# mLSTM cell and feed-forward on one core: another hand-written order for the first chunk

## The chip, the core and the metric

The kernel runs on one core of a Trainium2 chip. The metric is the device time of one execution in microseconds (us). Below, PE is TensorE (matrix products), DVE is VectorE, ACT is ScalarE, POOL is GpSimd, and SP is SyncE, which here only issues transfers (DMAs). All engines run their own queues in order and wait for each other on semaphores.

## What is computed

An mLSTM cell (a gated linear recurrence over 768 positions, for 4 batches of 8 heads of size 40) feeds a feed-forward layer with a leaky ReLU over the 3072 tokens. The recurrence is written step by step in the reference; the kernel computes it in chunks.

```python
for t in range(S):                                  # S = 768; B = 4, H = 8, D = 40
    m_new = np.maximum(f_gate[:, :, t] + m, i_gate[:, :, t])
    f_stab = np.exp(f_gate[:, :, t] + m - m_new)
    i_stab = np.exp(i_gate[:, :, t] - m_new)
    C = f_stab[..., None, None] * C + i_stab[..., None, None] * np.einsum('bhd,bhe->bhde', vt, kt)
    n = f_stab[..., None] * n + i_stab[..., None] * kt
    denom = np.maximum(np.abs(np.einsum('bhd,bhd->bh', n, qt)), 1.0)
    y[:, :, t] = o * np.einsum('bhde,bhe->bhd', C, qt) / denom
x = y.transpose(0, 2, 1, 3).reshape(3072, 320)
h = x @ w_in                                        # 320 x 2048
out = np.maximum(0.01 * h, h) @ w_out               # 2048 x 320
```

The feed-forward weights arrive as 64-bit floats, which the kernel narrows to 32 bits itself with a row of DVE instructions.

## The kernel before

The 768 positions are cut into 6 chunks of 128. A *step* `s` is one batch of one chunk: steps 0 to 3 are chunk 0, steps 4 to 7 chunk 1, and so on. The feed-forward of chunk `g` runs on PE while the cell work of chunk `g+1` is slipped in between its units.

**The first chunk** has no feed-forward to lie beside. Its order is written out by hand in the string `ORDER`. Each word is a call (table `acts_of` in `first_chunk`), and PE, DVE, ACT and POOL run their instructions exactly in the order in which the words issue them. SP's transfers stand in that order too. The words that matter here:

- `ld s`, `lo s`, `lw n`: load k, q, v of a step; its output gate; block `n` of w_in as 64-bit numbers (blocks 0 to 3 are w_in). `fd s` and `ll s i` load for later steps.
- `g c`, `ge c`, `ug c`: gates of chunk `c` on DVE (L297 to L317), their exponentials on ACT, their transposes on PE (L347, L352) with the copy on DVE (L357).
- `ab`, `abw s`: PE spreads gate rows over the partitions (L472), DVE adds the mask (L482).
- `tr s i`, `tc s i`: PE turns k (i = 0) or q (i = 1) of a step (L595), ACT copies the result out of PSUM (L601).
- `sc s`, `exp s`, `scm s`: scores on PE (L610), eight exponentials on ACT (L499), their product on DVE (L617). `vu`, `st`, `stc`: the new state on POOL, PE (L625) and DVE (L633).
- `val s`, `den s`, `gate s`, `gp s`: values on PE (L690), denominator on DVE (L682 to L684), output gate on DVE (L702), division on POOL (L719).
- `x s`, `xc s`: PE turns the token rows (L893), ACT copies them into `xT` (L906, L907).
- `nw n`: the next of seven instructions that narrow weight block `n`: L264 on ACT, then L266, L268, L270, L275, L279, L281 on DVE. `nw 0 e` narrows one half of block 0. The feed-forward may read a block after its L281.
- `ff j b0 b1`: feed-forward unit `j` for the batches `b0` to `b1-1`: ten products of 64x128 weights with 128 columns a batch (L924), then two leaky ReLUs on ACT (L932).
- `warm n`: `n` spare products of the identity with itself (L340); nobody reads them.

**The feed-forward of chunk 0** follows, interleaved with the cell of chunk 1, and is 30 units: units 0 and 1 finish `ff 0` and `ff 1` for batches 2 and 3, units 2 to 13 are pairs of half units for j = 2 to 7 (six and four products of 512 columns), and units 14 to 29 are the second layer (L960), four products each. So unit 6 is the first that reads weight block 2, and unit 10 the first that reads block 3; unit 14 reads the blocks 4 and 5 (w_out), unit 26 the blocks 10 and 11. Three tuples set what goes between the units: `PASSES[i]` gives how many narrowing instructions are issued before unit `i`; `fetch` gives the unit ahead of which further blocks of w_out are loaded; `place[n]` gives the unit behind which the n-th cell part of chunk 1 is issued. These parts are `u_parts` (turns, scores and state sums of a step: L559, L667, L672, L677) and `u_plain` (values of a step, hN at L730, then den, gate and state), for steps 4 to 7, the gate transposes of chunk 2, and the turning of the four token rows (`u_x1`, L893).

PSUM is two sets of four banks: the feed-forward, the masks and the spare products take turns in one, the cell in the other.

```python
            run(now, PASSES[i])
            for n in fetch.get(i, ()):
                load_weights(QN + n)
            ...
            exps()
            ffs[i]()
            ...
            while done < min(len(cells), sum(p <= i for p in place)):
```

Of the kernel before, what the change touches and what calls it, by code (L numbers as in the profile page):

```python
# [22 lines left out]
def kernel(  # L23
# [53 lines left out]
    gp = ctx.enter_context(tc.tile_pool(name="gates", bufs=1))  # L77
# [283 lines left out]
    st = {}  # L361
# [721 lines left out]
    def run(steps, n=None):  # L1083

        for _ in range(H if n is None else n):
            next(steps, None)
# [34 lines left out]
            nc.tensor.matmul(st["warm"][:], lhsT=ident[:], rhs=ident[:], start=True, stop=True)  # L1121

    ORDER = """
ld 0; g 0; ld 1; ge 0; lo 0; lw 0; warm 3; warm 4
lo 1; ld 2; warm 1; warm 5; warm 1; ab 0; ug 0; ld 3
abw 0; lo 2; tr 0 0; tr 1 0; tc 1 0; tr 1 1; tr 0 1; abw 1
tc 0 1; tc 0 0; warm 3; sc 0; vu 0; vu 1; vu 2; lo 3
lw 1; o 0; tc 1 1; st 1; st 0; stc 1; exp 0; stc 0
scm 0; exp 1; warm 6; warm 3; sc 1; warm 3; scm 1; ab 2
val 0; g 1; abw 3; tr 2 0; tr 2 1; val 1; tr 3 0; tiles  # L1130
den 0; nw 0 1; gate 0; nw 0 0; abw 2; tc 2 0; tc 2 1; ge 1
o 1; vu 3; tc 3 0; exp 2; warm 4; sc 2; ps 0; gp 0
ps 1; gate 1; nw 0 0; nw 0 0; den 1; scm 2; ug 1; nw 0 1
nw 0 1; o 2; tr 3 1; warm 4; val 2; x 0; tc 3 1; exp 3
nw 0 0; warm 3; st 2; xc 0; nw 1; gate 2; den 2; sc 3
stc 2; st 3; nw 0 0; nw 0 0; scm 3; nw 0 0; nw 0 1; fd 4
gp 2; ll 4 1; ps 2; gp 1; lw 2; warm 5; x 1; val 3
nw 0 1; xc 1; o 3; den 3; gate 3; nw 0 1; nw 0 1; nw 1
stc 3; nw 1; warm 3; ff 0 0 2; x 2; gp 3; lw 3; ps 3
fd 5; ll 5 1; ll 4 2; x 3; xc 2; xc 3; lw 4; ll 5 2  # L1140
lw 5; fd 6; nw 1; nw 1; nw 1; fd 7; lw 6; ff 1 0 2
sp 4; spc 4; nw 1
"""

    def first_chunk():

        ffs, narrow = [], {}

        def ff(j, b0, b1):
            if not ffs:  # L1150
                ffs.extend(ff_units(0))
            ffs[0](j, b0, b1)

        def step(n, e=None):
            if (n, e) not in narrow:
                narrow[n, e] = narrow_weights(n, e)
            next(narrow[n, e], None)

        acts_of = {
            "ld": load, "lo": load_o, "lw": load_weights, "g": gates, "ge": gates_exp, "warm": warm,  # L1160
            "ug": lambda c: gates_T(c, bus[c][0] if c == 0 else bus.pop(c)[0]),
            "tr": u_transpose, "tc": transpose_copy, "ab": lambda n: spread_first(bus[0][1], n), "abw": spread_mask,
            "exp": lambda n: run(prep_exp(n)), "vu": prep_vu, "tiles": prepare_tiles, "sc": u_scores, "scm": scores_mix,
            "st": state, "stc": state_copy, "val": u_values, "den": values_den, "o": prep_o, "gate": gate,
            "gp": gate_scale, "nw": step, "ps": prepare_step, "x": u_x, "xc": x_copy, "ff": ff,
            "sp": split_turn, "spc": split_copy, "warmer": warmer, "idle": idle, "fd": feed, "ll": load_late,
        }
        for line in ORDER.split("\n"):
            for what in line.split(";"):
                name, *args = what.split() or [None]  # L1170
                if name:
                    acts_of[name](*map(int, args))
        return ffs[1]

    E = mybir.EngineType
    with tc.manual_schedule(engines={E.PE, E.DVE, E.Activation, E.Pool}):
        ffs = first_chunk()
        fetch = {3: (3, 4), 13: (5, 6), 15: (7,)}
        PASSES = (5, 0, 3, 0, 0, 1, 7, 1, 0, 4, 3, 0, 1, 3, 10, 0, 1, 1, 3, 2, 9, 6, 0, 3, 3, 1, 7, 1, 2, 19)
        place = (1, 4, 8, 13, 15, 18, 20, 20, 23, 25, 26, 27, 27)  # L1180
        late = {}
        now = (None for n in range(2, QN + NF // 2) for _ in narrow_weights(n))

# [9 lines left out]
        for i in range(len(ffs)):  # L1193
            run(now, PASSES[i])
            for n in fetch.get(i, ()):
# [158 lines left out]
```

## Time and profile before

| | us |
|---|---|
| median of 3 runs | 481.94 (481.75 to 482.24) |
| the profiled execution | 481.68 |
| its span, first to last instruction | 479.5 |
| PE busy | 473.3 (99% of the span) |
| DVE busy | 365.6 (76%) |
| ACT busy | 199.9 (42%) |
| POOL busy | 162.1 (34%) |
| granted PE clock | 1.00 throughout |

What lies around the span is 481.68 - 479.5 = 2.2 us. By stages of the span:

| stage (us) | PE busy | DVE busy | ACT busy | POOL busy | share of the DMA engines |
|---|---|---|---|---|---|
| 0 to 10 | 8.20 | 5.03 | 2.27 | 5.10 | 0.73 |
| 10 to 20 | 9.51 | 6.55 | 8.04 | 0.85 | 1.02 |
| 20 to 30 | 10.00 | 8.22 | 8.43 | 5.90 | 0.98 |
| 30 to 40 | 9.74 | 9.44 | 5.28 | 4.17 | 0.84 |
| 40 to 50 | 10.00 | 9.72 | 9.65 | 5.92 | 1.10 |
| 60 to 70 | 10.00 | 9.77 | 7.75 | 6.99 | 0.67 |
| 110 to 120 | 9.35 | 9.63 | 2.80 | 2.58 | 0.52 |
| 130 to 140 | 10.00 | 1.69 | 3.01 | 0.00 | 0.44 |

A busy PE does not mean a useful one: the spare products count as busy. In a line of the timeline the first number is the start, the second how long the group took, `x16` how many instructions it merges, and the bracket the idle time before it and who ended it. A PE product of 32-bit numbers is recorded as two matmuls (so four products of `warm` are x8); a turn is one.

### The profile page before, as it was taken

Reading aid. Unit: us, or ns where it says so; the run is one execution under the profiler, and the core shown is the slowest. Engines: PE = TensorE matmul, PEld = TensorE weight load, DVE = VectorE, ACT = ScalarE, POOL = GpSimd, SP = SyncE. Lnnn points to the kernel's source line nnn. Section 1 sums busy time; section 2 is a strip of 40 time slices with the busy share of each in tenths; the row PEclk is TensorE's granted clock in tenths of the full one; section 3 lists DMA queues with packets and bytes.
Section 4 is the critical chain, followed back from the end, with each engine's and each line's share of the span. In section 5 each row is a group of like instructions: output and inputs, shape, how many; then the busy total and the mean of one; then the engine's idle time right before and its main releaser. Section 6 shows DMA issues by size and latency. Waiting matters only on the chain.

```text
span 479.5 us, 12091 instructions
## 1 busy us (share of the span) xinstructions
PE 473.3 (99%) x4753; PEld 370.2 (77%) x4753; DVE 365.6 (76%) x601; ACT 199.9 (42%) x523; POOL 162.1 (34%) x209
## 2 busy tenths in 40 slices
PE   8999999999999999999999999999999999999997
PEld 7998745776655599955469985548998899988997
DVE  4789999999916899787987958889899968335611
ACT  3787874663732422315151222524025642156310
POOL 4156251342603637554641735462310002000020
PEclk9999999999999999999999999999999999999999
DMA  7989869975636785777777868773250030100001
GB/s 151 182 161 228 196 122 261 233 186 127 141 90 135 166 180 150 158 174 179 149 167 156 227 161 190 182 171 114 80 212 29 1 109 1 52 7 1 7 9 41
DMA packets 142600, 63.36 MB, mean 132 GB/s; under 512 B 110480, under 2 KB 130768, under 8 KB 142544
## 3 DMA queue, kind: packets, MB, share of 16 engines
q1 hardware_dynamic: 142160, 62.47, 55.7%
q8 instruction: 37, 0.61, 0.5%
q14 instruction: 19, 0.16, 0.1%
q10 hardware_dynamic: 384, 0.13, 0.1%
HBM read 51.68 MB, written 8.27 MB: 125 GB/s over the span
## 4 chain that ended last, share of the span: by engine, by line
PE 89%; DVE 6%; DMA 2%; ACT 1%; issue 1%; POOL 1%; SPq 0%; ACTq 0%; DVEq 0%; POOLq 0%
PE po L999 32%; PE ph L924 29%; PE ph L850 8%; PE pe L850 4%; PE pT L760 3%; PE sd L667 3%; PE po L960 2%; PE pa L690 2%; PE warm L340 1%; DVE w_out L281 1%; DVE w_out L279 1%; PE sd L672 1%; DMA qn<-in_q_dram 1%; PE sc L610 1%; PE tkq L595 1%
## 5 line engine op out<-in xcount | busy, mean ns | idle before, releaser
L924 PE MATMUL ph<-xT,w_in 64*128 64x512 f32 (+1 forms) x680 | 142.0, 569 | 0.0
L924 PEld LDWEIGHTS ph<-xT,w_in 64*128 64x128 f32 x680 | 67.7, 187 | 64.2 <-issue 61.3
L999 PE MATMUL po<-w_out,acts 128*128 128x160 f32 x640 | 90.2, 300 | 0.0
L999 PEld LDWEIGHTS po<-w_out,acts 128*128 128x128 f32 x640 | 87.4, 190 | 1.9 <-ACT w L499 0.8
L932 ACT ACTIVATE acts<-ph 128x512 f32<-128x512 f32 (+1 forms) x68 | 35.1, 567 | 81.6 <-PE ph L924 81.5
L499 ACT ACTIVATE w<-w,gT 128x64 f32<-128x64 f32 (+1 forms) x192 | 51.7, 348 | 29.2 <-POOL w L491 27.2
L645 POOL TENSOR_TENSOR S<-S,f 40x336 f32<-40x336 f32 x36 | 36.4, 1010 | 77.8 <-PE pT L760 50.1
L999 PE MATMUL po<-raw,acts 128*128 128x160 f32 x320 | 45.1, 299 | 0.0
L1037 POOL TENSOR_TENSOR y<-y,raw 128x160 f32<-128x160 f32 x10 | 6.3, 633 | 112.6 <-ACT y L1036 112.6
L999 PEld LDWEIGHTS po<-raw,acts 128*128 128x128 f32 x320 | 44.0, 190 | 0.0
L677 DVE TENSOR_TENSOR qn<-w,sd 64x512 f32<-64x512 f32 x40 | 27.4, 684 | 17.8 <-PE sd L672 11.6
L960 PE MATMUL po<-w_out,acts 128*128 128x320 f32 x128 | 36.4, 436 | 0.6 <-DVE w_out L281 0.6
L872 DVE SCALAR_TENSOR_TENSOR acts<-ph,acts 128x512 f32<-128x512 f32 x32 | 20.6, 685 | 20.6 <-ACT acts L870 20.6
L551 DVE TENSOR_TENSOR qn<-kqT,late 64x512 f32<-64x512 f32 x32 | 35.0, 1093 | 1.0
L491 POOL TENSOR_TENSOR w<-w,i 128x512 f32<-128x512 f32 x20 | 32.1, 1605 | 10.7 <-DVE S L649 9.9
L960 PEld LDWEIGHTS po<-w_out,acts 128*128 128x128 f32 x128 | 23.6, 190 | 10.0 <-DVE w_out L281 1.2
L774 POOL TENSOR_TENSOR xb<-xb,den 128x320 f32<-128x320 f32 x16 | 11.6, 727 | 47.8 <-DVE xb L771 47.8
L870 ACT ACTIVATE acts<-pe 128x512 f32<-128x512 f32 x32 | 17.4, 595 | 19.0 <-PE pe L850 18.9
L778 DVE STREAM_TRANSPOSE x<-xb 128x512 f32<-128x512 f32 x16 | 17.7, 1107 | 7.7 <-POOL xb L774 7.7
L667 PEld LDWEIGHTS sd<-kqT 40*64 40x64 f32 x640 | 19.6, 135 | 5.0 <-issue 4.8
L876 ACT ACTIVATE acts<-acts 128x512 f32<-128x512 f32 x32 | 19.7, 633 | 8.1 <-DVE acts L872 8.1
L999 PE MATMUL po<-raw 128*128 128x160 f32 x160 | 22.8, 300 | 0.0
(167 smaller groups left out, 771.0 us busy)
## 6 DMA issues: line engine op xcount, KB each, us to landing
w<-a_dr SPq DMA_DIRECT2D x40, 128.0 KB, 3.8
rb<-in_k_dram SPq DMA_DIRECT2D x64, 80.0 KB, 2.8
rb<-in_q_dram SPq DMA_DIRECT2D x64, 80.0 KB, 2.6
rb<-in_o_gate_dram SPq DMA_DIRECT2D x64, 80.0 KB, 2.6
xT<-x_dr SPq DMA_DIRECT2D x32, 160.0 KB, 3.3
late<-a_dr SPq DMA_DIRECT2D x32, 128.0 KB, 3.5
x_dr<-x SPq DMA_DIRECT2D x16, 256.0 KB, 3.1
kn<-in_k_dram SPq DMA_DIRECT2D x24, 160.0 KB, 4.1
```

The costliest lines, as they stand in the source:

```text
L491: nc.gpsimd.tensor_tensor(w, w, cm2.unsqueeze(1).to_broadcast([P, H, SL]), op=ALU.add)
L499: yield nc.scalar.activation(w[:, h, :], w[:, h, :], AF.Exp, bias=gT[c][:, 0, bh : bh + 1], scale=1.0)
L551: nc.vector.tensor_tensor(mixed(s)[rows, 1 - r], d["kqT"][rows, 1].rearrange("p (h t) -> p h t", t=SL), d["ea"][rows], op=ALU.mult,)
L645: nc.gpsimd.tensor_tensor(new, old, g, op=ALU.mult)
L667: nc.tensor.matmul(bank[1 - u][toks, h, :], lhsT=kqT[rows, 0, ts(h, SL)], rhs=kqT[rows, 1, ts(h, SL)], start=True, stop=True,)
L677: nc.vector.tensor_tensor(mixed(s)[toks, u], w[toks], bank[1 - u][toks], op=ALU.mult)
L850: nc.tensor.matmul(ph[r][:], lhsT=parts["w", key][n][part, at : at + P], rhs=xs[key][part, slot, :], start=start and slot == 0, stop=stop ...
L872: nc.vector.scalar_tensor_tensor(fs[r], in0=ph[r][:], scalar=1.0 + EPS, in1=fs[r], op0=ALU.mult, op1=ALU.add,)
L924: nc.tensor.matmul(ph[r][:, cols], lhsT=w_row(r, slot, j), rhs=xT[DP * r : DP * (r + 1), slot, bs, :], start=(slot == 0), stop=(slot == KC ...
L932: nc.scalar.activation(acts[:, f, cols], ph[r][:, cols], AF.Prelu, alpha=0.01)
L960: nc.tensor.matmul(po[n][:], lhsT=acts[:, f, ts(n, P)], rhs=w_out[:, f, :], start=(f == 0), stop=(f == NF - 1),)
L999: nc.tensor.matmul(bank[:], lhsT=left[:, f, :], rhs=right[:, f, :], start=f == 0, stop=f == KH - 1)
```

## The change

Only the string `ORDER` and the three tuples change. In the order, k and q of step 1 are loaded before those of step 0, the loads of step 2 are moved ahead of an output gate, step 0 and 1 are turned as k1, k0, q0, q1 and copied as q0, k1, q1, k0, and the narrowing instructions, divisions and copies of the later steps stand at other places. `ff 0 0 2` becomes `ff 0 0 1` and `ff 0 1 2`: the unit's ten products of 256 columns become twenty of 128. The spare products are 44 where they were 48. The loads of step 5 (`fd 5`) now stand ahead of `lw 3`. Among the units, `u_plain` of step 4 moves from unit 4 to 5, `u_parts` of step 5 from unit 8 to 10, and the turns of the token rows from units 25, 26, 27, 27 to 24, 25, 25, 28.

```diff
--- before.py
+++ after.py
@@ -1121,25 +1121,25 @@
             nc.tensor.matmul(st["warm"][:], lhsT=ident[:], rhs=ident[:], start=True, stop=True)
 
     ORDER = """
-ld 0; g 0; ld 1; ge 0; lo 0; lw 0; warm 3; warm 4
-lo 1; ld 2; warm 1; warm 5; warm 1; ab 0; ug 0; ld 3
-abw 0; lo 2; tr 0 0; tr 1 0; tc 1 0; tr 1 1; tr 0 1; abw 1
-tc 0 1; tc 0 0; warm 3; sc 0; vu 0; vu 1; vu 2; lo 3
-lw 1; o 0; tc 1 1; st 1; st 0; stc 1; exp 0; stc 0
-scm 0; exp 1; warm 6; warm 3; sc 1; warm 3; scm 1; ab 2
-val 0; g 1; abw 3; tr 2 0; tr 2 1; val 1; tr 3 0; tiles
-den 0; nw 0 1; gate 0; nw 0 0; abw 2; tc 2 0; tc 2 1; ge 1
-o 1; vu 3; tc 3 0; exp 2; warm 4; sc 2; ps 0; gp 0
-ps 1; gate 1; nw 0 0; nw 0 0; den 1; scm 2; ug 1; nw 0 1
-nw 0 1; o 2; tr 3 1; warm 4; val 2; x 0; tc 3 1; exp 3
-nw 0 0; warm 3; st 2; xc 0; nw 1; gate 2; den 2; sc 3
-stc 2; st 3; nw 0 0; nw 0 0; scm 3; nw 0 0; nw 0 1; fd 4
-gp 2; ll 4 1; ps 2; gp 1; lw 2; warm 5; x 1; val 3
-nw 0 1; xc 1; o 3; den 3; gate 3; nw 0 1; nw 0 1; nw 1
-stc 3; nw 1; warm 3; ff 0 0 2; x 2; gp 3; lw 3; ps 3
-fd 5; ll 5 1; ll 4 2; x 3; xc 2; xc 3; lw 4; ll 5 2
-lw 5; fd 6; nw 1; nw 1; nw 1; fd 7; lw 6; ff 1 0 2
-sp 4; spc 4; nw 1
+warm 3; g 0; warm 9; warm 1; ld 1; warm 1; ld 0; lo 0
+lw 0; ge 0; ld 2; lo 1; ab 0; ld 3; abw 0; lo 3
+lo 2; tr 1 0; ug 0; tr 0 0; tr 0 1; tr 1 1; abw 1; tc 0 1
+tc 1 0; tc 1 1; tc 0 0; warm 7; sc 0; vu 1; vu 0; vu 2
+tiles; lw 1; st 1; st 0; stc 1; exp 0; o 0; scm 0
+stc 0; exp 1; warm 3; sc 1; warm 3; warm 2; scm 1; ab 2
+val 0; nw 0 1; abw 3; g 1; tr 2 0; tr 2 1; val 1; tr 3 0
+abw 2; gate 0; nw 0 0; den 0; nw 0 0; tc 2 1; ge 1; o 1
+tc 2 0; gate 1; nw 0 0; tc 3 0; den 1; gp 0; ps 1; vu 3
+ps 0; exp 2; warm 3; sc 2; nw 0 1; scm 2; ug 1; o 2
+warm 3; tr 3 1; x 0; val 2; tc 3 1; nw 0 0; xc 0; nw 0 0
+exp 3; o 3; gate 2; nw 0 1; warm 4; st 2; nw 1; den 2
+sc 3; st 3; stc 2; scm 3; nw 0 0; fd 4; gp 1; nw 0 0
+nw 0 1; ps 2; gp 2; ll 4 1; lw 2; warm 2; nw 0 1; x 1
+val 3; xc 1; gate 3; den 3; nw 0 1; nw 0 1; stc 3; nw 1
+nw 1; warm 3; ff 0 0 1; ff 0 1 2; x 2; gp 3; fd 5; lw 3
+ps 3; ll 5 1; ll 5 2; ll 4 2; x 3; xc 2; xc 3; lw 4
+lw 5; fd 6; fd 7; nw 1; lw 6; ff 1 0 2; sp 4; nw 1
+nw 1; spc 4; nw 1
 """
 
     def first_chunk():
@@ -1175,9 +1175,9 @@
     E = mybir.EngineType
     with tc.manual_schedule(engines={E.PE, E.DVE, E.Activation, E.Pool}):
         ffs = first_chunk()
-        fetch = {3: (3, 4), 13: (5, 6), 15: (7,)}
-        PASSES = (5, 0, 3, 0, 0, 1, 7, 1, 0, 4, 3, 0, 1, 3, 10, 0, 1, 1, 3, 2, 9, 6, 0, 3, 3, 1, 7, 1, 2, 19)
-        place = (1, 4, 8, 13, 15, 18, 20, 20, 23, 25, 26, 27, 27)
+        fetch = {2: (3, 4), 16: (7,), 5: (5, 6)}
+        PASSES = (6, 0, 2, 1, 1, 2, 6, 0, 0, 1, 0, 2, 4, 3, 7, 2, 1, 0, 5, 3, 5, 4, 0, 8, 1, 1, 2, 0, 1, 28)
+        place = (1, 5, 10, 13, 15, 18, 20, 20, 23, 24, 25, 25, 28)
         late = {}
         now = (None for n in range(2, QN + NF // 2) for _ in narrow_weights(n))
```

## The prediction

> **What bounds the kernel now.** I read first who PE waits for (us in total, times, longest), since PE is busy for 99% of the span:
>
> ```profile
> PE warm L340 <- POOL ident masks.py:199: 1.5, 1, 1.5
> PE po L960 <- DVE w_out L281: 0.6, 1, 0.6
> PE sc L610 <- ACT kqT L601: 0.5, 1, 0.5
> PE tkq L595 <- DMA qn<-in_q_dram: 0.3, 1, 0.3
> PE xt L893 <- POOL x L719: 0.2, 1, 0.2
> ```
>
> PE stands still for 1.6 us between its start and its end. So a new order gains by doing less on PE (spares), or by these waits, and it can lose anywhere. Next the chain that ended last (start, us, what), around the second line:
>
> ```profile
> 70.23 10.50 PE ph L924 x48
> 80.73 1.11 PE hN L730 x32
> 81.87 0.18 DVE den L682
> ...
> 117.63 0.83 DVE w_out L281
> 118.51 1.34 PE po L960 x4
> ```
>
> To 81.8 the chain is PE, from there to 118.5 almost all DVE, then PE again. Two queues set the end of the first chunk and lie within 0.6 us of each other. After that PE never waits until its last 3 us, and DVE idles from 131.8 to 141.6 until PE releases it, so a shift of PE at 127 should reach the end whole. Last the timelines of PE, DVE and POOL:
>
> ```profile
> 11.50 1.16 PE L610 MATMUL sc<-kqT 40*128 40x128 f32 x16 [0.49 <-ACT kqT L601]
> 23.60 1.06 PE L340 MATMUL warm<-ident 128*128 128x128 f32 x8
> 37.58 2.43 PE L924 MATMUL ph<-xT,w_in 64*128 64x256 f32 x20
> ...
> 32.14 0.78 DVE L275 TENSOR_SCALAR w_in<-acts 128x640 uint32<-128x640 uint32 x1
> 32.95 0.82 DVE L279 SCALAR_TENSOR_TENSOR w_in<-acts,w_in 128x640 f32<-128x640 uint32 x1
> 33.81 1.28 DVE L617 TENSOR_TENSOR w<-w,sc 128x512 f32<-128x512 f32 x2
> ...
> 47.59 1.49 DVE L281 SCALAR_TENSOR_TENSOR w_in<-w_in,late 128x1280 f32<-128x1280 f32 x1
> 68.38 2.44 DVE L281 SCALAR_TENSOR_TENSOR w_in<-w_in,late 128x1280 f32<-128x1280 f32 x1
> 81.87 0.17 DVE L682 TENSOR_SCALAR den<-hN 128x8 f32<-128x8 f32 x1 [0.60 <-PE hN L730]
> ...
> 67.73 1.74 POOL L491 TENSOR_TENSOR w<-w,i 128x512 f32<-128x512 f32 x1 [0.74 <-DMA w<-a_dr]
> ```
>
> Three prices are in it. A spare product is two of the x8, 0.22 us. Products of 128 columns that alternate between two row halves cost 1.09 us for eight (11.50 to the next start at 12.59), 0.136 each. And the same L281 takes 1.49 us alone and 2.44 beside POOL.
>
> **The change, step by step.** The instructions are the old ones but for four spares less (-0.9 us of PE), ten products of 256 columns turned into twenty of 128, and two ReLUs made four halves (some 0.5 us of ACT, ahead of the copies of `xT`). I follow starts, old and new; new ones are sums of the old durations.
>
> *0 to 18 us.* The fifth transfer is q of step 0 now, q of step 1 before; it lands at 9.2 either way. Four copies of 0.48 us then stand ahead of `sc 0`, not three: 9.85 + 4 x 0.48 + 0.1 = 11.9, 0.45 later; seven spares fill it. Behind, three spares stand ahead of `sc 1` instead of nine, so it is held by the first half of `scm 0` (15.07) and starts at 15.1, not 15.54. `exp 1` still ends near 16.95, so `scm 1` stays at 16.8. Nothing gained on DVE, 0.1 on PE.
>
> *18 to 36 us.* DVE waits 0.4 us for the masks, which stand ahead of `g 1`. ACT begins `exp 2` at 24.1 (24.34 before), behind the copy of k3, so `scm 2` is at 26.3 (26.52). Turning x of step 0 ahead of `val 2` lets `gate 2` follow the values at once: 29.75, not 30.25. An L275 now fills the hole that DVE had there, and an L279 is put behind `scm 3`. The copies `xc 0` go ahead of `exp 3` on ACT, so `exp 3` ends at 32.0 instead of 30.0; DVE reaches `scm 3` at 31.9 (33.81), so that delay is just covered. `gp 1`, which PE waited 0.25 us for, is done near 29, not 34.4. `val 3` starts at 33.2 (34.82).
>
> *36 to 44 us.* Three spares, then `ff 0 0 1` from 35.95. By the rows, its twenty products cost 2.73 us where the ten cost 2.36 (37.58 to 39.94): +0.4. The nearest row has the same geometry, alternating halves of the array; the other end is the spare's 0.22, 4.4 us, +2.1. x of steps 2 and 3 comes to 38.7, `ff 1` to 39.5, `sp 4` to 41.9, and unit 0 to **42.9 against 44.13: -1.2**. Its last copy of `xT` (L907) is done at 42.9 by eight ACT copies of 0.44 behind x. DVE ends block 1 (L281) at about 48.1, against 49.08.
>
> *The loads.* `fd 5`, seven transfers, passes `lw 3` on SP's queue. Before, block 3 landed from 46.8 to 50.7 and the seven from 52.0 to 55.9. Swapped, 5.3 us of transfers go first: block 3 lands near 56. Its L264 stands at the head of ACT's queue at about 53, so ACT stands still until then; behind it are the ReLUs of units 3 and 5 and the exponents of step 5. PE needs the first of these banks at 60.0, and they come at 58.5: covered by 1.5 us. The cover ends when block 3 lands after 57.
>
> *Unit 10.* `u_parts` of step 5 moves behind it, so unit 10 comes 1.6 us earlier (a turn and the sums, 68.50 to 70.16) on top of the 1.2: at 68.8, not 71.9 less waits. It needs block 3's L281, which ended at 70.82. This is the tight spot. With the old durations DVE, 0.95 earlier, ends it at 69.9: a wait of 1.1. But POOL's division for step 4 now waits for a `gate` that DVE issues behind L270, L275 and L279 of block 3; the POOL work of 62.1 to 67.0 follows it and no longer lies beside those three, which took 1.90, 1.39 and 1.89 there and 1.49, 0.82 and 1.48 on block 2. That is 1.4 us off, so 68.5: no wait. I take 0.3.
>
> *81 to 127 us.* `den` of step 5 waits for hN and moves by -1.2 + 0.3 = -0.9. DVE's 36.6 us behind it hold the same instructions, so the last L281 ends at 118.46 - 0.9 = 117.56. PE's product that needs it would have come at 117.74 without the wait; now two triples of turns (0.33 each) stand ahead of it: 117.74 - 0.9 + 0.66 = 117.5. Both arrive together, and the 0.7 us lost there is filled with turns. From there to the next feed-forward took 8.72 (118.51 to 127.23), now 8.06: 117.6 + 8.06 = 125.7 against 127.23, **-1.6 us**. The four spares are inside this, not beside it.
>
> 481.68 - 1.6 = 480.1 for the profiled execution. The median lies 0.26 above it, so 480.3.
>
> **The rivals.**
>
> *Half-width products cost full price.* For it: the spares, whose weights fill the whole array, take 0.11 us a record and no less. Against it: `sc`, 0.068 a record. At 4.4 us unit 0 comes at 44.6, +0.5; unit 10 then finds its weights ready, and the end is 117.74 + 0.5 + 0.66 + 8.06 = 126.96, -0.3: 481.7. Much the same follows if `exp 3`, moved behind the copies, holds DVE up by a microsecond and POOL's work costs what it did: block 3 ends at 70.9, unit 10 starts there and not at 70.3 (its old time less the 1.6 us moved behind it), hN is 0.6 later, DVE's last L281 at 119.1, and 119.1 + 8.06 = 127.2: no change.
>
> [...]
>
> *Block 3 lands late.* SP took 2.0, 2.6 and 2.7 us to issue three transfers of v for step 5 beside full queues (42.8 to 50.2). If that holds back `lw 3`, ACT stays shut behind its L264 and DVE has no block 3. From 57.3 on every microsecond goes to unit 10 one to one: landing at 58.9 undoes the gain, at 60.5 it costs 1.6 more: 483.5. Against it: the transfers that filled the queue were `lw 3` itself.
>
> *Unit 10 doesn't wait, nor anything else:* -1.9, 480.0. It is the end of my forecast's range.
>
> That the order does not hold is no rival: the queues are in order.
>
> **How the numbers follow.** Forecast, -1.0 to -2.1 (unit 10 waits 0 to 1.0): 0.57, at 480.3, own range 479.8 to 480.9. Half-width or `exp 3`, -0.9 to +0.4 (the parts between their ends): 0.26. Late block 3, up to +3: 0.17. A measurement of this kernel tells 0.2%, 1.0 us, from no change. Faster than 481.0: 0.57 and a little of the second, 0.60. Slower than 482.9: most of the third, 0.13. The rest, 0.27, is the same. The range 479.7 to 482.3 leaves out the late block's upper part (0.13) and a little below the forecast's best edge (0.03).
>
> **What would show it.** `sc 0` at 11.9; DVE's third L702 at 29.8; twenty `ph` products of 128 columns in 2.7 us; unit 0's start at 42.9; L281 of block 3 at 68.5 to 69.9 with little idle time of PE ahead of unit 10; no PE wait for L281 near 117; the 30 products of chunk 1's feed-forward starting at 125.7. A PE wait for DVE of over 1 us at 69, or a line of PE waiting for ACT's ReLUs at 60, would make it wrong.

## The result, and the profile after

| | before | after |
|---|---|---|
| median of 21 runs each (us) | 481.75 (481.31 to 482.29) | 480.81 (479.97 to 481.54) |
| ratio, 95% interval | | 0.9979 (0.9973 to 0.9985) |
| span of the profiled execution | 479.5 | 478.6 |
| PE busy | 473.3 | 473.6 |
| DVE busy | 365.6 | 367.7 |

The change gains 0.94 us, 0.2%, clear of the noise; the forecast was 1.6. What PE waits for (us in total, times, longest), in the changed kernel:

```profile
PE warm L340 <- POOL ident masks.py:199: 1.5, 1, 1.5
PE ph L924 <- DVE w_in L281: 0.2, 1, 0.2
```

Four of the five waits of before are gone, the 0.6 for the last L281 among them; one of 0.2 is new. Yet DVE is busy for 2.1 us more with the same 601 instructions. The chain that ended last (start, us, what) in the changed kernel, where PE used to wait:

```profile
117.39 0.84 DVE w_out L281
118.27 5.65 PE po L960 x20
```

DVE and PE meet at 118.2, DVE still last by a hair. The timelines of PE and DVE of the changed kernel (start, length, what, and in brackets the idle time ahead):

```profile
7.01 1.28 PE L472 MATMUL ab<-a,ident 32*128 32x128 f32 x32
12.28 1.16 PE L610 MATMUL sc<-kqT 40*128 40x128 f32 x16
36.73 2.50 PE L924 MATMUL ph<-xT,w_in 64*128 64x128 f32 x40
40.23 2.43 PE L924 MATMUL ph<-xT,w_in 64*128 64x256 f32 x20 [0.19 <-DVE w_in L281]
116.24 0.38 PE L893 MATMUL xt<-ident,x 128*128 128x128 f32 x2
116.56 0.38 PE L893 MATMUL xt<-ident,hn 128*128 128x128 f32 x2
116.89 7.03 PE L960 MATMUL po<-w_out,acts 128*128 128x320 f32 x24
...
29.28 1.29 DVE L275 TENSOR_SCALAR w_in<-acts 128x640 uint32<-128x640 uint32 x1
30.57 0.72 DVE L702 SCALAR_TENSOR_TENSOR x<-acts,pa 128x320 f32<-128x320 f32 x1
32.96 1.29 DVE L617 TENSOR_TENSOR w<-w,sc 128x512 f32<-128x512 f32 x2 [0.22 <-PE sc L610]
66.99 1.68 DVE L281 SCALAR_TENSOR_TENSOR w_in<-w_in,late 128x1280 f32<-128x1280 f32 x1
81.69 0.16 DVE L682 TENSOR_SCALAR den<-hN 128x8 f32<-128x8 f32 x1
```

The forty half-width records run from 36.73 to the next start at 39.16: 2.43 us. The turns at 116.24 and 116.56 now stand ahead of the products for which PE used to wait. And `ab` begins at 7.01, not at 6.60 as before, though 14 spares stand ahead of it in both.

The start of `ab` is a trap: the 28 spare records ahead of it start 0.213 us apart at first and 0.112 apart later, and the pace changed at 5.26 in the profile of before, at 6.11 in this one. In the 14 profiles of this case, all with the same 14 spares ahead, `ab` began anywhere from 6.29 to 7.74. So I compare steps by their distance from the second `ab` (17.50 before, 17.85 after), with the starts, for L281 the ends:

| us behind the second `ab` | before | after | difference | forecast |
|---|---|---|---|---|
| unit 0 | 26.63 | 25.76 | -0.87 | -1.2 |
| L281 of block 1 ends | 31.58 | 31.54 | -0.04 | -0.95 |
| L281 of block 3 ends | 53.32 | 50.82 | -2.50 | -0.9 to -2.3 |
| hN of step 5 | 63.17 | 62.34 | -0.83 | -0.9 |
| `den` of step 5 | 64.37 | 63.84 | -0.53 | -0.9 |
| last L281 ends | 100.96 | 100.37 | -0.59 | -0.9 |
| second feed-forward | 109.73 | 108.49 | -1.24 | -1.6 |

The start of the second feed-forward settles the time: from there to the end of the span it is 352.3 us in all 14 profiles.

### The profile page after: what moved, and what is told of

It is laid out like the page before. It is cut to its first block, busy times and chain, and to the rows that moved or that the text cites. A ratio compares the mean times of both kernels' runs of the same rounds, so it can differ in the third digit from the quotient of the medians.

```text
span 478.6 us, 12120 instructions
## 1 busy us (share of the span) xinstructions
PE 473.6 (99%) x4765; PEld 368.4 (77%) x4765; DVE 367.7 (77%) x601; ACT 199.9 (42%) x525; POOL 159.8 (33%) x209
## 4 chain that ended last, share of the span: by engine, by line
PE 75%; SPq 12%; DMA 7%; DVE 2%; POOL 1%; issue 1%; ACT 1%; ACTq 0%; DVEq 0%; POOLq 0%
PE po L999 32%; PE ph L924 22%; PE ph L850 8%; PE pe L850 4%; PE pT L760 3%; SPq L373 3%; PE sd L667 3%; DMA S<-in_v_dram 2%; SPq L231 2%; SPq L422 2%; PE po L960 2%; DMA acts<-in_moe_w_in_dram 2%; DMA raw<-in_moe_w_out_dram 2%; SPq L375 1%; SPq L438 1%
## 5 line engine op out<-in xcount | busy, mean ns | idle before, releaser
L924 PE MATMUL ph<-xT,w_in 64*128 64x512 f32 (+2 forms) x700 | 141.9, 557 | 0.2 <-DVE w_in L281 0.2
L924 PEld LDWEIGHTS ph<-xT,w_in 64*128 64x128 f32 x700 | 65.7, 187 | 66.5 <-issue 64.1
L932 ACT ACTIVATE acts<-ph 128x512 f32<-128x512 f32 (+2 forms) x70 | 35.3, 555 | 78.3 <-PE ph L924 78.2
L645 POOL TENSOR_TENSOR S<-S,f 40x336 f32<-40x336 f32 x36 | 32.7, 908 | 80.1 <-PE pT L760 49.4
L491 POOL TENSOR_TENSOR w<-w,i 128x512 f32<-128x512 f32 x20 | 31.5, 1574 | 5.4 <-ACT acts L932 5.4
```

Of the source, the lines that this page charges most:

```text
L491: nc.gpsimd.tensor_tensor(w, w, cm2.unsqueeze(1).to_broadcast([P, H, SL]), op=ALU.add)
L645: nc.gpsimd.tensor_tensor(new, old, g, op=ALU.mult)
L924: nc.tensor.matmul(ph[r][:, cols], lhsT=w_row(r, slot, j), rhs=xT[DP * r : DP * (r + 1), slot, bs, :], start=(slot == 0), stop=(slot == KC ...
L932: nc.scalar.activation(acts[:, f, cols], ph[r][:, cols], AF.Prelu, alpha=0.01)
```

## Experiments

Times are medians; ratios are to the kernel before, run in the same series.

**Which half of the change carries the gain.** The order of the first chunk with the old tuples:

```diff
-        fetch = {2: (3, 4), 16: (7,), 5: (5, 6)}
-        PASSES = (6, 0, 2, 1, 1, 2, 6, 0, 0, 1, 0, 2, 4, 3, 7, 2, 1, 0, 5, 3, 5, 4, 0, 8, 1, 1, 2, 0, 1, 28)
-        place = (1, 5, 10, 13, 15, 18, 20, 20, 23, 24, 25, 25, 28)
+        fetch = {3: (3, 4), 13: (5, 6), 15: (7,)}
+        PASSES = (5, 0, 3, 0, 0, 1, 7, 1, 0, 4, 3, 0, 1, 3, 10, 0, 1, 1, 3, 2, 9, 6, 0, 3, 3, 1, 7, 1, 2, 19)
+        place = (1, 4, 8, 13, 15, 18, 20, 20, 23, 25, 26, 27, 27)
```

> The new order of the first chunk with the old tuples (passes, fetches, places). My theory: the gain of 0.9 us is two parts, 0.5 us by which PE comes earlier to unit 0 (43.6 instead of 44.1) and a wait of 0.8 us near 117 that two triples of turns fill. Here the second part is missing: the second feed-forward starts 0.2 to 0.4 us earlier than before (126.8 to 127.0), the time is 481.3 to 481.6, and a wait of PE for a DVE L281 of 0.6 to 1.0 us stands near 117. Rival, the order carries it all: 480.8, start at 126.3. Second rival, the order is only good with its own tuples, because block 3 now lands at 58: PE waits for it at unit 8 to 10, and the time is 482 to 483.

Measured 481.01, 0.3 us below what I had, ratio 0.9991 (0.9980 to 1.0002): not told apart from no change. Its profile is of an execution of 481.98, 1.0 us above its median. The waits of PE in it:

```profile
PE ph L924 <- ACT acts L932: 0.9, 1, 0.9
PE po L960 <- DVE w_out L281: 0.6, 1, 0.6
```

The second line is what I expected. The first is the late block: with the old places ACT's L264 of block 3, 57.78 here, shuts in ReLUs that PE needs at 65.0, and the second feed-forward starts at 127.90. So the second rival of this run also has its share, at 0.9 us in this execution, though the median is not the 482 to 483 us that it named. The other half, the new tuples on the old order:

> The old order of the first chunk with the new tuples. My theory: PE comes to unit 0 at 44.1 as before, DVE's last L281 near 117 stays within 0.3 us of 118.5, but the wait there is filled by turns: the second feed-forward starts 0.4 to 0.7 us earlier than before (126.5 to 126.8), the time is 481.1 to 481.4. Rival, the order carries it all: 481.7, no change. Rival, the tuples carry it all: 480.8.

480.98, ratio 0.9984 (0.9975 to 0.9992), 0.1 us below what I had. By the ratios the tuples alone bring 0.16%, the order alone 0.09%, which may be nothing, and both together 0.21%. So the tuples alone already gain, and the rival that they carry it all (480.8) is not excluded: their interval overlaps that of the whole change (0.9973 to 0.9985). What the new order adds is seen in the traces (with the old order unit 0 comes 26.64 us behind the second `ab`, where the changed kernel has 25.76), but not shown in the time.

**The turns that fill the wait.** The changed kernel with the old end of `place`, and the old kernel with the new end:

```diff
-        place = (1, 5, 10, 13, 15, 18, 20, 20, 23, 24, 25, 25, 28)
+        place = (1, 5, 10, 13, 15, 18, 20, 20, 23, 25, 26, 27, 27)
```

> The changed kernel with the four turns of the token rows put back behind units 25, 26, 27, 27. My theory: the wait of PE for the last L281 near 117 returns with 0.4 to 0.8 us, the second feed-forward starts at 126.8 to 127.1, the time is 481.3 to 481.5. Rival: the turns only lie elsewhere and DVE has no part in it, time 480.8 and no wait in the record.

```diff
-        place = (1, 4, 8, 13, 15, 18, 20, 20, 23, 25, 26, 27, 27)
+        place = (1, 4, 8, 13, 15, 18, 20, 20, 23, 24, 25, 25, 28)
```

> The kernel before with only the four turns of the token rows moved to behind units 24, 25, 25, 28. My theory: they fill the wait of 0.63 us for the last L281 near 117 (two triples of 0.33 us more ahead of it), 0.5 to 0.65 us gained, second feed-forward at 126.6 to 126.8, time 481.1 to 481.25. Rival: the turns ahead of unit 26 wait for the values of step 7 or for their copies themselves, or the products that follow them wait for a bank: nothing gained, 481.7.

With the turns put back: 481.57, ratio 0.9993 (0.9985 to 1.0002), two thirds of the gain lost, about 0.7 us, and PE's wait is there again:

```profile
PE po L960 <- DVE w_out L281: 0.8, 1, 0.8
```

The turns alone on the old kernel: 483.41, ratio 1.0050 (1.0033 to 1.0066), slower, against my expectation. PE's longest wait, in its timeline:

```profile
119.62 0.41 PE L893 MATMUL xt<-ident,hn 128*128 128x128 f32 x2 [2.56 <-DVE hn L741]
```

By this releaser the third turn takes a PSUM bank whose last reader is L741 of step 7 (the row that it turns is that of step 6, long done), and DVE issues that L741 behind the very L281 the turns were to cover (118.83 to 119.48). In the changed kernel the same turn takes a bank that an ACT copy of a token row released at 116.0. So filling this wait was worth 0.7 us only with the rest of the tuples.

**The split and the late block.** One piece again:

```diff
-nw 1; warm 3; ff 0 0 1; ff 0 1 2; x 2; gp 3; fd 5; lw 3
+nw 1; warm 3; ff 0 0 2; x 2; gp 3; fd 5; lw 3
```

> The changed kernel with the first unit again in one piece: ten products of 256 columns where it has twenty of 128. My theory: forty half-width records take 2.43 us in the changed kernel and twenty of 256 columns 2.36 us, so the split costs 0.07 us; x of step 1 is copied by then, so nothing waits: 480.6 to 481.0, as the changed kernel. Rival one, half-width products cost full price: the unit is 1.9 us shorter and the time 479 to 480. Rival two, the split lets the unit start before x of step 1 is copied: without it PE waits 0.3 us or more for ACT, 481.2 or more.

481.10, ratio 0.9987 (0.9978 to 0.9996), not told apart from the changed kernel, and 0.1 us above what I had. Unit 0 came 31.05 us behind the start of `sc 0`, 31.33 in the changed kernel and 31.15 in the kernel with the turns put back, and no wait appeared: the split buys and costs next to nothing.

Block 3 loaded first again:

```diff
-nw 1; warm 3; ff 0 0 1; ff 0 1 2; x 2; gp 3; fd 5; lw 3
+nw 1; warm 3; ff 0 0 1; ff 0 1 2; x 2; gp 3; lw 3; fd 5
```

> The changed kernel with the loads of block 3 put back ahead of the loads of step 5. Rival of the prediction, block 3 lands late (57.9) and holds ACT or DVE: with its landing back at 50 to 52 the time falls by 0.3 to 1.0 us, to 479.8 to 480.5. My theory: the late landing is covered, so nothing is gained by it; what the swap moves is POOL's L491 of step 5, which follows the loads of step 5: from 51.0 back to 56, beside DVE's L281 of block 2, which then takes 2.4 us and not 1.5. DVE ends block 3 some 0.5 to 1 us later (69.2 to 69.7 at the same start), the time is 480.8 to 481.5.

480.69, ratio 0.9972 (0.9960 to 0.9984), six runs: no difference from the changed kernel. Block 3 landed at 52.8 where it had landed at 57.9. ACT's timeline, here and then in the changed kernel:

```profile
53.42 1.38 ACT L264 ACTIVATE late<-raw 128x1280 bf16<-128x1280 bf16 x1
```

```profile
58.03 1.38 ACT L264 ACTIVATE late<-raw 128x1280 bf16<-128x1280 bf16 x1 [5.06 <-DMA raw<-in_moe_w_in_dram]
```

ACT stands still for 5 us in the changed kernel and it costs nothing there. The move of POOL's L491 came, to 57.37, and DVE's L281 beside it took 1.85 us, where I had 2.4, and not 1.48; block 3's L281 ended only 0.2 us later, counted from the second `ab`.

**What POOL costs DVE.**

```diff
         w = st[s]["w"]
+        if s == B:
+            return
         nc.gpsimd.tensor_tensor(w, w, cm2.unsqueeze(1).to_broadcast([P, H, SL]), op=ALU.add)
...
         d = st[s]
+        if s == B:
+            return
         nc.gpsimd.tensor_tensor(
             mixed(s)[:, 0, :, :D], natural(s, 1), gT[c][:, 2, ts(b, H)].unsqueeze(2).to_broadcast([P, H, D]), op=ALU.mult,
...
+        if s == B and u == 0:
+            return
         nc.gpsimd.tensor_tensor(new, old, g, op=ALU.mult)
```

> The changed kernel without three instructions of POOL for step 4 (the mask added to w, q times its gate, the old state times its factor: L491, L527, L645; what is computed for chunk 1 lacks them). In the changed kernel they lie at 40.5 to 43.7, beside L266, L268 and L270 of block 1, which take 1.35, 0.89 and 1.95 us there. My theory, POOL's tensor operations slow DVE's: without them these three take about 0.5, 0.5 and 1.5 us, and block 1's L281 ends 0.8 to 1.4 us earlier against the start of the scores of step 0. Of that little reaches the end, because at 81 DVE is only 0.2 us later than PE's hN: time 480.4 to 480.8. Rival: the durations belong to the instructions' place (other causes, such as the loads then running) and stay at 1.3, 0.9 and 1.9 us.

480.38, ratio 0.9970 (0.9958 to 0.9982). The timelines of POOL and DVE in the changed kernel, where the three lie beside block 1:

```profile
40.55 1.27 POOL L491 TENSOR_TENSOR w<-w,i 128x512 f32<-128x512 f32 x1
41.77 0.98 POOL L527 TENSOR_TENSOR qn<-rb,gT 128x320 f32<-128x320 f32 x1
42.83 0.90 POOL L645 TENSOR_TENSOR S<-S,f 40x336 f32<-40x336 f32 x1
43.80 1.85 POOL L519 TENSOR_TENSOR vu<-kn,gT 128x320 f32<-128x320 f32 x1
...
40.82 1.35 DVE L266 TENSOR_SCALAR late<-late 128x1280 bf16<-128x1280 bf16 x1
42.21 0.89 DVE L268 TENSOR_SCALAR late<-late 128x1280 uint16<-128x1280 uint16 x1
43.13 1.94 DVE L270 SCALAR_TENSOR_TENSOR late<-acts,late 128x1280 uint16<-128x1280 uint16 x1
45.00 1.34 DVE L275 TENSOR_SCALAR w_in<-acts 128x1280 uint32<-128x1280 uint32 x1
```

And without the three (L521 is the L519 of the changed kernel):

```profile
40.93 0.72 POOL L521 TENSOR_TENSOR vu<-kn,gT 128x320 f32<-128x320 f32 x1
...
41.20 0.81 DVE L266 TENSOR_SCALAR late<-late 128x1280 bf16<-128x1280 bf16 x1
42.04 0.49 DVE L268 TENSOR_SCALAR late<-late 128x1280 uint16<-128x1280 uint16 x1
42.56 1.49 DVE L270 SCALAR_TENSOR_TENSOR late<-acts,late 128x1280 uint16<-128x1280 uint16 x1
43.98 0.82 DVE L275 TENSOR_SCALAR w_in<-acts 128x1280 uint32<-128x1280 uint32 x1
48.67 0.49 DVE L266 TENSOR_SCALAR late<-late 128x1280 bf16<-128x1280 bf16 x1 [0.82 <-ACT late L264]
```

The four took 5.52 us beside POOL and take 3.61 here: 1.9 us of DVE, so the durations belong to POOL and not to the place. Block 1's L281 ends 35.84 us behind `sc 0`, 1.3 earlier than in the changed kernel (37.11); I had 0.8 to 1.4. In the time this is not told apart from the changed kernel. The last line shows one place where it is lost: DVE, now early, waits 0.82 us for block 2's load. But the profile is of the slowest of the five executions (481.10), in which block 2 landed at 46.9 and block 3 at 58.9, where the changed kernel's profile has 45.0 and 57.9; so how much of the 1.3 us could reach the end stays open.

**What still holds the first chunk.** In the changed kernel DVE stands still 0.78 us at 18.3 for the masks of the second `ab`, with five spares ahead of it on PE:

```diff
-stc 0; exp 1; warm 3; sc 1; warm 3; warm 2; scm 1; ab 2
+stc 0; exp 1; warm 3; sc 1; scm 1; ab 2
```

> The changed kernel without the five spare products that stand between the scores of step 1 and the masks of steps 2 and 3 (ab 2). In the changed kernel these masks start 1.3 us after the scores end, and DVE stands idle 0.78 us for them at 18.3. My theory: DVE is the bound from here to 50, so masks 1.2 us earlier close this hole, everything behind it on DVE and PE comes 0.6 to 0.8 us earlier, and the time is 480.0 to 480.4. Rival one: the next thing late takes over at once (the loads of k2 and q2 at 18.7 and 19.3, block 0 at 18.5): no gain, 480.6 to 481.0. Rival two: PE without spares idles and its clock falls: slower than 481.2, and a granted clock below 1 at 16 to 25.

481.02, ratio 0.9983 (0.9974 to 0.9992): rival one, with a trace of rival two: in three of the twelve executions the granted clock was 0.996, and these took 481.4 to 482.3 us; a fourth had 0.975 and took 490.6. The ratio leaves that fourth out; the median of the other eleven is 480.83. DVE's timeline, at the masks and at `scm 3`:

```profile
18.45 1.41 DVE L482 TENSOR_TENSOR w<-ab,cmask 128x256 f32<-128x256 f32 x4
...
32.95 0.69 DVE L617 TENSOR_TENSOR w<-w,sc 128x512 f32<-128x512 f32 x1 [0.73 <-ACT w L499]
```

The hole at 18 is closed and one of 0.73 us has opened at `scm 3`, where ACT is late. What takes over is not one of the loads I had named: ACT stands 1.77 us at `o 2` for an output gate that landed at 28.16, behind that of step 3. So the two loads were swapped, first alone and then without the five spares too:

```diff
-lw 0; ge 0; ld 2; lo 1; ab 0; ld 3; abw 0; lo 3
-lo 2; tr 1 0; ug 0; tr 0 0; tr 0 1; tr 1 1; abw 1; tc 0 1
+lw 0; ge 0; ld 2; lo 1; ab 0; ld 3; abw 0; lo 2
+lo 3; tr 1 0; ug 0; tr 0 0; tr 0 1; tr 1 1; abw 1; tc 0 1
```

> The changed kernel with the loads of two output gates swapped: lo 2 ahead of lo 3. In the changed kernel lo 2 lands last of the two, at 25.1 to 28.7 in four profiles, and ACT stands at o 2 for it for 0 to 1.85 us, ahead of the copies of x and of exp 3; DVE has a hole of 0.2 to 1.1 us at scm 3 for it. My theory: with lo 2 landing at 24.4 to 25.8 ACT does not wait, the hole at scm 3 is gone, and the time falls by 0.2 to 0.6 us: 480.2 to 480.6. Rival: the hole is filled by something else (the narrowing of block 1 waits for its load at 33 instead), 480.7 to 481.0.

> Both: lo 2 ahead of lo 3, and the five spares ahead of ab 2 left out. Without the spares alone DVE's hole at 18.3 went, and one of 0.73 us at scm 3 came in its place, because ACT stood 1.77 us at o 2 for its transfer; nothing was gained. My theory: with that transfer earlier the gain is kept: scm 3 starts 0.6 to 1.0 us earlier against the scores of step 0 (20.7 us behind them in the changed kernel, now 19.7 to 20.1), and the time is 479.8 to 480.3. Rival: further on DVE meets the transfers of block 1 (33) and of block 2, which do not move: 480.6 to 481.0.

Alone: 481.10, ratio 0.9983 (0.9974 to 0.9992), no gain. The hole at `scm 3` was 0.22 us, as in the changed kernel. Together: 480.32, ratio 0.9967 (0.9956 to 0.9979), and `scm 3` starts 19.66 us behind `sc 0` (20.68 in the changed kernel). In the trace the two edits only work together: alone they bring `scm 3` 0.3 and 0.1 us nearer to `sc 0`, together 1.0. In the time, the interval of both together still overlaps those of each alone and of the change. What then holds DVE, from its timeline:

```profile
59.49 0.49 DVE L266 TENSOR_SCALAR late<-late 128x1280 bf16<-128x1280 bf16 x1 [0.69 <-ACT late L264]
```

That is block 3, landing at 57.95: once the rest is a microsecond earlier, the late block bites, 0.69 us on DVE and 0.5 on PE.

Last the start: copies in the order of the turns, two spares and not seven ahead of `sc 0`, on top of both edits, and then with the five spares back:

```diff
-lo 3; tr 1 0; ug 0; tr 0 0; tr 0 1; tr 1 1; abw 1; tc 0 1
-tc 1 0; tc 1 1; tc 0 0; warm 7; sc 0; vu 1; vu 0; vu 2
+lo 3; tr 1 0; ug 0; tr 0 0; tr 0 1; tr 1 1; abw 1; tc 1 0
+tc 0 0; tc 0 1; tc 1 1; warm 2; sc 0; vu 1; vu 0; vu 2
```

> As the kernel with both, and the copies of k and q of steps 0 and 1 in the order in which they are turned (k1, k0, q0, q1 where the changed kernel copies q0, k1, q1, k0), with two spares ahead of the scores of step 0 in place of seven. In the changed kernel ACT begins the copies only when q0 is turned, 3.2 us behind the start of ab; k1 is turned 1.3 us before that. My theory: the start is a chain PE, ACT, PE, with no transfer in it; the copies end some 0.9 us earlier, the scores of step 0 start 4.2 to 4.6 us behind ab and not 5.3, and the time falls by 0.4 to 0.9 us against the kernel with both: 479.0 to 479.8. Rival: v of step 2 (lands 20.2), block 0 (18.5) and the output gates then set the pace: no gain against the kernel with both.

> As the kernel with lo 2 first and the copies in the order of turning, with the five spares ahead of ab 2 put back. Without them that kernel took 479.0 to 480.7 us in seven executions and 481.7 to 485.5 in five, and the five had a granted PE clock of 0.986 to 0.993 where the others had 0.999 to 1.000. In its profile PE turned q2 at 19.40, 0.1 us behind the landing of q2 (19.26), at a late start (ab at 7.65). My theory: in executions that start up to 1.4 us earlier PE stands still there for the transfers, and the clock falls for it; the five spares (1.3 us) keep PE behind the transfers, so no execution has a clock below 0.996, and the time is 480.0 to 480.6 (DVE's hole of 0.78 us at 18 returns, the earlier start of 1.3 us against ab stays in part). Rival: the clock falls for the spares taken away ahead of the scores of step 0; then it still falls in about four executions of ten.

With both edits: 480.60, ratio 0.9997 (0.9969 to 1.0026), unclear, since the executions fall into two groups (below). With the five spares back: 479.94, ratio 0.9961 (0.9946 to 0.9976), granted clock 1.000 in all five executions: the best of all kernels here, though its interval still touches that of the change. Its start in PE's timeline:

```profile
7.54 1.28 PE L472 MATMUL ab<-a,ident 32*128 32x128 f32 x32
11.48 1.16 PE L610 MATMUL sc<-kqT 40*128 40x128 f32 x16
```

`sc 0` begins 3.94 us behind `ab`, 5.27 in the changed kernel: my theory had 4.2 to 4.6.

## Why the prediction held, and where it missed

The time, 480.81, lies 0.5 us above the forecast and just inside its own range. Part of that is luck: the range stood on a median before of 481.94, from 3 runs, and the 21 runs of the result have 481.75. As a change, -0.94 falls just short of the forecast's -1.0 to -2.1. (The far end of that range is 0.2 us beyond the -1.9 worked out for no wait; no step of the sum gives it.) In kind the mechanism was the one forecast: PE reaches unit 0 earlier, DVE's holes ahead of it close, and turns fill the wait near 117. In size the step that failed most is DVE up to the end of block 1 (0.04 us gained, not 0.95); the split and block 3 did better than forecast. Point by point:

*The start: right for an equal `ab`.* `sc 0` was forecast at 11.9, from `ab` at 6.60. The changed kernel puts it 5.27 us behind `ab` whenever q has landed: 11.87. What I did not see is that the old order has slack there and the new one hardly any:

| profile | first `ab` | `sc 0` | distance |
|---|---|---|---|
| before | 6.60 | 11.50 | 4.90 |
| old order, turns moved | 7.11 | 11.45 | 4.34 |
| old order, new tuples | 7.74 | 12.08 | 4.34 |
| new order, turns back | 6.29 | 11.60 | 5.31 |
| new order, POOL's three left out | 6.38 | 12.01 | 5.63 |
| new order, block 3 first | 6.47 | 12.03 | 5.56 |
| new order, old tuples | 6.50 | 11.77 | 5.27 |
| after | 7.01 | 12.28 | 5.27 |
| new order, one piece | 7.69 | 12.96 | 5.27 |

At an early `ab` the old order waits for a transfer and for ACT (0.34 and 0.49 us in its profile), so up to about 7.1 a late `ab` costs it nothing; in the new order the delay goes into `sc 0` one to one, unless q lands late, as in the rows with 5.63 and 5.56 (q of step 0 at 9.16 and 9.19, just after PE was ready to turn it). The gain thus depends on the execution: -1.24 us from the second `ab` on, less what the start gives back (0.35 in this pair of profiles). The median's 0.94 fits that.

*18 to 36: the holes closed, longer instructions took the time.* From DVE's first copy of a state, at 13.22 and 14.00, to the end of block 1's L281, at 49.08 and 49.39, its holes fell from 3.61 to 2.03 us, 1.6 gained; its busy time rose from 32.25 to 33.36, 1.1 lost. The 0.5 that is left only makes up for the first copy, which now comes 0.43 later, counted from the second `ab`. The L275 put into the hole ahead of `gate 2` took 1.29 us, beside POOL's division (29.05 to 29.96), where the row quoted of before has 0.78, and `gate 2` came at 30.57, not 29.75; 0.35 of this is the later start. The scan L297 at 20.38 took 0.94 beside POOL's L509, 0.41 before. That POOL makes them longer is shown by leaving its work out only for block 1; for these two it is read from the overlap. This is the step that failed: I counted POOL's work where it moved off block 3, and nowhere that it moved to. So block 1's L281 came 0.04 us earlier, not 0.95.

*The split: right, and cheap.* 2.43 us where I had 2.73 and the other end 4.4. The trace decides against the spare's price, 0.22 us a product, for products that alternate between the halves. Its records start in pairs 0.007 us apart, with a new pair every 0.112, the pace of the spares' single records: I read a pair as one record of each half, side by side, so that two of them cost what one spare record costs.

*36 to 44.* Unit 0 gained 0.87, not 1.2. Counted from the second `ab`, `ff 0 0 1` began 1.20 earlier where the forecast had 1.63. PE was busy for all of the 18.88 us between the two: what it gained there is the wait of 0.25 and eight records of spares less, 0.9 at 0.11 each. The forecast had walked from DVE's `scm 3` to `val 3` without adding up PE's own instructions. The split cost 0.07 where it had 0.37; and 0.27 went ahead of `ff 1`, where PE waits for an L281 (0.19 in its line).

*The loads.* Block 3 landed at 57.9, past the 57 at which I said the cover ends and later than the 56 I expected, and PE lost nothing: ACT's ReLUs came at 60.5, and PE, itself later than forecast, reached the group that needs them at 60.96 and not at 60.0. With block 3 back at 52.8 nothing was gained. So the rival of the late block fell here, but its place was right: it cost 0.9 us with the old tuples and 0.5 in the kernel that is a microsecond faster.

*Unit 10: right.* Block 3's L281 ended at 68.67 (forecast 68.5), since POOL no longer lay beside L270, L275 and L279 (1.49, 0.82, 1.49 as forecast). PE did not wait.

*81 to 127: right in kind, half in size.* hN came 0.83 us earlier, but `den` only 0.53: DVE came to it at 81.7, last instead of PE, because POOL now lay beside the w_out instructions of 68.6 to 73 (L275 1.56 us, 0.49 otherwise). The chain "`den` waits for hN" no longer held. The wait at 117 is filled as forecast, and from the last L281 to the next feed-forward it is 8.12 us (forecast 8.06).

*The rivals.* Half-width at full price is refuted. `exp 3`, moved behind the copies, does not hold DVE in this profile: the line of `scm 3` has a hole of 0.22 us, and the bracket names PE's scores of step 3, not ACT. Where the output gate of step 2 landed late, at 28.2 us and after, `exp 3` did hold it, by 0.34, 0.73 and 1.09 us in three runs: the delay that I called just covered is covered only when that transfer is early.

## What to carry to other kernels

When a hole on one engine is filled by moving instructions, price them by what the neighbour engines do at the new place, not by their old duration: here 1.6 us of closed holes came with 1.1 us of slower instructions. Compare two profiles from an event behind the first spares, not from zero: `ab` behind the same 14 spares began 1.45 us apart in 14 profiles. And a filler edit belongs to the schedule that it was found with: the same four turns were worth 0.7 us in one and cost 1.8 us in the other, where one of them had to wait for a PSUM bank.

## What the runs showed of the hardware

**Overlaps of POOL and DVE.** The two timelines above can be read almost to the tenth. L266 starts at 40.82 while POOL's L491 runs to 41.82: 1.00 of waiting and 0.48 of its own (its time at 60.09) would make 1.48, the record says 1.35. L270 starts at 43.13, L645 runs to 43.73: 0.60 + 1.49 (its time without the three) = 2.09, recorded 1.94. And POOL's L519, 0.72 without the three, takes 1.85 behind that L270, which ends at 45.07: 45.07 + 0.72 = 45.79, recorded 45.65. So in these three overlaps one instruction seems to wait for the other's end and then to take its own time, rather than both running slowly; the records agree with that within 0.15 us. By that reading each of the three cost what was left of the instruction that began first. What makes one wait for the other, no trace here shows. Not every overlap is like this: DVE's L702 at 25.14, which reads PSUM, took 0.72 us beside POOL's L719 (25.08 to 25.82), where the four L702 of the trace take 0.70 to 0.73. Why, no run shows.

**The pace of the first spares.** With the same 14 spares the start of `ab` lay 1.45 us apart in 14 profiles (6.29 to 7.74). What differs is how many of the 28 records start 0.213 us apart before the others start 0.112 apart: 18 in the profile of before, 22 in that of the changed kernel, and all 28, up to 7.4 us, in the one with `ab` at 7.74. For the one with `ab` at 6.29 I estimate 15, and the change of pace at 4.6: its `ab` is 0.31 us earlier than that of before, and a record at the faster pace saves 0.10. The granted clock reads 1.00 on both sides of the change in the profiles of before and after, so they do not show what changes the pace, nor why it changes at another time in another execution.

**Executions with a lower granted clock.** In the old kernel with the turns moved, PE stands still for 2.6 us near 117. Six of its executions had a granted clock of 0.999 to 1.000 and took 482.9 to 483.5 us; four had 0.996 and took 485.1 to 485.5, 2 us more, which is what 0.4% of the span comes to. No listed execution of the kernel before or of the changed kernel lies below 0.999. That the standstill brings the clock down is not shown: the run without the five spares has three executions at 0.996 and one at 0.975, the run with the unit in one piece one at 0.996 (482.8 us), and in their profiles PE has no wait above 0.2 us behind its start. The kernel with the copies and both edits, ten spares fewer than the changed kernel, had 0.999 to 1.000 in seven executions (479.0 to 480.7) and 0.986 to 0.993 in five (481.7 to 485.5). In its profile PE turned q2 0.1 us behind its landing. With the five spares ahead of the second `ab` back, none of five executions fell. That would fit PE waiting there for a transfer in the executions that fell; but the kernel with both edits lacks these five as well, and none of its five fell. None of the fallen executions has a profile, so where PE stood still in them, if it did, stays open.
